# Attention and two mixture layers: filler products in the first head pairs, a common PSUM buffer for a product with phi, a later operand split, and transposes taken together

## The chip, the cores and the metric

The kernel runs on one core of one Trainium2 chip. What is measured is the device time of one execution in microseconds (us). The core has five engines with queues of their own: TensorE (PE in the rows, PEld for its weight loads), VectorE (DVE), ScalarE (ACT), GpSimd (POOL) and SyncE (SP), which here issues the transfers. 1.05 us is 0.2% of this kernel's time.

## The reference

Three layers follow each other: attention with a block-causal mask, a dense layer with a bent activation, and a soft mixture of eight experts with 32 slots in all.

```python
scores = scale * q @ k.T                          # 4 batches x 8 heads, 576 rows, head size 64
scores = where(row_block >= col_block, scores, -1e9)   # blocks of 64
x = softmax(scores) @ v                           # -> x: 2304 x 512
h = x @ w_in                                      # 512 x 2048
g = where(h >= 1, h, where(h <= -1, 0, (h + 1) ** 2 / 4))
x = g @ w_out                                     # 2048 x 512
logits = x @ phi                                  # 512 x 32
d = softmax(logits, over the tokens)
slot_input = d.T @ x                              # 8 experts x 4 slots x 512
slot_out = maximum(slot_input @ w1, 0) @ w2       # per expert, 512 x 1024 and 1024 x 512
out = softmax(logits, over the slots) @ slot_out
```

## The kernel before

**Attention** (about 0 to 200 us). There are 16 head pairs (a batch and two heads). The string `PLAN` is an order written out by hand: each of its tokens is a step of a pair, with a digit that says how many pairs behind the newest one it runs. Steps that matter here: `sc` are the score products of one row block (L113 for the diagonal one, L120 for the others), `mk` adds the mask to them with two small products (L126), `mx` takes the maximum on VectorE, `ex` the exponentials on ScalarE (L151), `no` scales the rows on GpSimd (L163), `pt` transposes them on TensorE (L171), `pc` copies them out. Scores lie in the PSUM pool `psc` (tag `sc`, two buffers of two banks), the transposes in the pool `ptr` (tag `tr`, three buffers of one bank).

**Blocks** (about 200 to 459 us). The tokens are five blocks, four of 512 and one of 256. `Moe.run` goes through a list of units k = 0, 1, ...; unit (b, f) computes 128 of the 2048 columns of h for block b: 12 products (L538, three for each of four parts of x, because both operands are split into a high and a low part), in a buffer of `ptr`, followed by the activation. The activation reads the buffer on ScalarE and last on VectorE (the maximum, L573), which frees it. The first 21 units alternate between blocks 0 and 1; then come 16 units each of block 2 (k = 21 to 36), 3 (37 to 52) and 4 (53 to 68). What else is done beside the units stands in a plan by unit:

- `w_parts` splits a tile of w_in into its two parts: a cast on ScalarE, then a subtraction and an addition on GpSimd (L484, L485). The tile is wanted by unit k's products some units later: w7 to w15 are made this way during the first units.
- `split(2)` splits x of block 2 in two halves, each a cast on ScalarE (L409) and two subtractions on GpSimd (L412). The first half is made ahead of the units, the second at k = 1 (`parts[1]()`).
- `wo_turn` transposes one tile of w_out (L498) in half of the buffer `aside`, which holds one of the two `psc` buffers through most of the block stage; ScalarE copies it out. After four tiles, `wo_phi` multiplies them with phi (L507, 16 products of 32 columns) and `wo_back` transposes the result (L516), both in that same half of `aside`, each with a copy by ScalarE (L511, L517). They run inside a unit, at k = 25 and 26, 30 and 31, 35 and 36, 40 and 41.
- `half(b, q, u)` transposes half u of a quarter of g of block b (L593, a `psc` buffer, copied out by ScalarE); with the second half of a quarter go its logits (`lt`, L613). `slots` multiplies them with the weights of the slots (L658), `soft`, `disp`, `weigh`, `maximum`, `weights` and `total` are the softmax pieces around it.
- `feed` issues the weights of the experts for the last stage as buffers come free.

**Experts** (about 459 to 521 us). A chain of small steps gives the slots' inputs, then the experts' two products run over weights that arrive by DMA. TensorE issues small filler products in its gaps there (L1015, bf16 128x128 zero operands).

The two places that the change touches first read:

```python
pairs[i].step(u)                      # L294
ps = self.aside[:, 1]                 # wo_phi and wo_back
if k == 1:
    parts[1]()
```

Of the kernel before, what the change touches and what calls it, by code (L numbers as in the profile page):

```python
# [7 lines left out]
F32 = mybir.dt.float32  # L8
# [6 lines left out]
P = 128  # L15
# [223 lines left out]

FILL = ""  # L240
WARM = 44

# [3 lines left out]
def attention(e, tc, nb=4, wl=(1, 1 + 2 * READY)):  # L248
    nc = tc.nc
    e.ENG = ENG  # L250

    def copy(eng, dst, src):
        if eng == "A":
            nc.scalar.copy(dst, src)  # L254
        elif eng == "D":
            nc.vector.tensor_copy(dst, src)
        else:
            nc.gpsimd.tensor_scalar(out=dst, in0=src, scalar1=1.0, scalar2=1.0, op0=ALU.mult, op1=ALU.mult)
    e.copy = copy
    e.eng = lambda c: nc.vector if c == "D" else nc.gpsimd  # L260

    e.QD, e.pr, e.v_, e.acc = [], [], [], []
    for i in range(2):
        e.QD.append(e.apool.tile([P, 2, P], F32R, tag=f"QD{i}", bufs=1, name=f"QD{i}"))
        z = (nc.gpsimd, nc.vector)[i]
        z.memset(e.QD[i][0:64, :, 64:P].bitcast(F32), 0.0)
        z.memset(e.QD[i][64:P, :, 0:64].bitcast(F32), 0.0)
        e.pr.append([e.apool.tile([P, P * (b // 2 + 1)], F32, tag=f"pr{i}{b}", bufs=1, name=f"pr{i}{b}")
                     for b in range(9)])
        z.memset(e.pr[i][8][:, 576:640], 0.0)  # L270
        e.v_.append(e.apool.tile([P, 5, 2, 64], F32, tag=f"natv{i}", bufs=1, name=f"vn{i}"))
        z.memset(e.v_[i][64:P, 4], 0.0)
    for i in range(2):
        e.acc.append(e.apool.tile([P, 16, 2], F32, tag=f"acc{i}", bufs=1, name=f"ac{i}"))
        nc.vector.memset(e.acc[i], 1e-9)
    e.low = e.apool.tile([P, P], mybir.dt.bfloat16, tag="low", bufs=1, name="low")
    e.one = e.apool.tile([P, 64], mybir.dt.bfloat16, tag="one", bufs=1, name="one")
    nc.vector.memset(e.low, 0.0)
    nc.vector.memset(e.one, 1.0)
    for h in (0, 64):  # L280
        nc.vector.memset(e.low[h:h + 1, 0:64], -2.0 ** 127)
    pairs = [Pair(e, nc, b, p) for b in range(nb) for p in range(4)]
    n = len(pairs)
    plan = [(it - int(u[0]), u[1:]) for it in range(n + 6) for u in PLAN.split()]
    plan = [(i, u) for i, u in plan if ((i, int(u[2:])) in EARLY if u[0] == "h" and u[1] in "mxyzoa" else
                                        0 <= i < n if u[0] != "w" else wl[0] <= i < wl[1])]
    fill = [(int(u[0]), u[1:]) for u in FILL.split()]
    assert sorted(fill) == sorted(plan[:len(fill)])
    for i, u in fill + plan[len(fill):]:
        if u[0] == "h":  # L290
            e.moe.early(u[1], *EARLY[i, int(u[2:])])
        elif u[0] != "w":
            pairs[i].step(u)
        else:  # L294
            t, c = (i - wl[0]) // 2, slice((i - wl[0]) % 2 * 256, (i - wl[0]) % 2 * 256 + 256)
            if u == "w0" and c.start == 0:
                e.moe.w_raw(t)
            elif u == "w1":
                e.moe.w_mul(t, c)
                e.moe.w_bits(t, c)  # L300
            elif u == "w2":
                e.moe.w_parts(t, c, e.ENG["w"])
# [14 lines left out]
class Moe:  # L317
# [183 lines left out]

    def wo_phi(self, c):
        e, nc = self.e, self.nc
        ps = self.aside[:, 1]
        for kk in range(4):
            for i in range(4):
                nc.tensor.matmul(ps[32 * i:32 * i + 32, 0:P], e.phi[:, kk], self.wT[2 * c + i // 2][:, i % 2, kk],  # L507
                                 start=(kk == 0), stop=(kk == 3))
        self.drop(f"wT{4 * c}", f"wT{4 * c + 2}")
        wp = self.wp = e.y[:, 3]  # L510
        nc.scalar.copy(wp, ps[:, 0:P])  # L511

    def wo_back(self, c):
        e, nc = self.e, self.nc
        ps = self.aside[:, 1]
        nc.tensor.transpose(ps[:, 0:P], self.wp, e.ident)  # L516
        nc.scalar.copy(e.w2p[:, 4 * c:4 * c + 4].rearrange("p i s -> p (i s)"), ps[:, 0:P])  # L517

# [311 lines left out]
    def plan_sides(self, at_unit):  # L830
# [6 lines left out]
        def put(k, name, *a):  # L837
            at.setdefault(k, []).append((name, *a))
            return k
        for f in range(16):  # L840
            k = put(prep[first + f] + 2, "wo_turn", f)
            if f % 4 == 3:
                c = f // 4
# [11 lines left out]
            put(free + 2 * b + 2, "weigh", b)  # L855
        free += 2
        at_half = {}
        for b in range(2, 4):
            for q in range(4):
                for u in range(2):  # L860
                    free = put(max(free + 1, pos(b, 4 * q + 3) + 2), "half", b, q, u)
                    at_half.setdefault((b, q), free)
            if b == 2:
                put(free, "soft", 2)
                for i, step in enumerate((("disp", 2), ("weigh", 2), ("logits", 3, range(8)))):
                    put(free + 1, *step)
                for i, step in enumerate((("slots", 2, 0), ("logits", 3, range(8, 16)), ("soft", 3))):
                    put(free + 2, *step)
                put(free + 3, "slots", 2, 1)
                put(free + 4, "disp", 3)  # L870
                put(free + 6, "maximum")
                put(free + 7, "weights")
                put(free + 8, "weigh", 3)
        put(at_half[3, 1] + 2, "slots", 3, 0)
        put(free + 1, "slots", 3, 1)
        put(free + 2, "total")
        for q in range(3):
            k = put(max(pos(4, 4 * q + 3) + 3, free + 1 + q), "half", 4, q, 0)
        put(k, "gather")
        for b in range(2, 5):  # L880
            for u, fn in enumerate(self.split(b)):
# [11 lines left out]
    def run(self):  # L893
# [23 lines left out]
        for k, (b, f) in enumerate(units):  # L917
            for i in [READY + n for n, p in enumerate(prep) if p == k - 1]:
                self.w_parts(i)
            for i in [READY + n for n, p in enumerate(prep) if p == k > 0]:  # L920
                self.w_mul(i)
                self.w_bits(i)
            if k == 1:
                parts[1]()
            for i in [READY + n for n, p in enumerate(prep) if max(p - 2, 0) == k and n > 1]:
                self.w_raw(i)
            self.h_unit(b, f, at.pop(-k, ()) if k else ())
            self.act_unit(b, f, "D" if k > prep[-1] or k < 18 and k % 2 else "A")
            for fn, *a in at.pop(k, []):
                (getattr(self, fn) if isinstance(fn, str) else fn)(*a)  # L930
            if k == 66:
                self.n4 = self.new([P, 4, 256], F32R, "n4")
                for i in range(4):
                    self.comb_parts(i)
            if k == 57:
                self.middle, self.spare = len(self.tape), 1
            if k > 29:
                self.feed()
# [306 lines left out]
```

## Time and profile before

| | |
|---|---|
| median of 3 runs | 523.71 us (523.31 to 523.95) |
| the profiled execution | 523.28 us |
| its span, first to last instruction | 521.5 us |
| TensorE busy | 500.6 us (96%) |
| VectorE, ScalarE, GpSimd busy | 331.6, 327.0, 203.9 us |
| mean granted clock of TensorE | 0.980 |

The profile is one execution. TensorE is busy nearly all the time, so the time is read from three things: where it waits (the view of the waits and the timeline), at which granted clock it works (the column PEclk of a stretch; 1.00 is 2.4 GHz, 0.50 is 1.2 GHz), and how many products it has. The timeline gives for each instruction its start, its length and, in brackets, the idle time of the engine before it and what ended that.

### The profile page before, as it was taken

What the parts mean: (1) busy time and instruction counts of PE and PEld (TensorE: products, weight loads), DVE (VectorE), ACT (ScalarE), POOL (GpSimd) and SP (SyncE); (2) the same over time, 40 slices, a digit from 0 to 9 for tenths busy, and PEclk for the clock granted to TensorE, in tenths of its full rate; (3) what the DMA queues carried; (4) which work ended last, traced back from release to release, by engine and by line L of the source; (5) the groups of instructions that cost most, each with busy time, mean ns of one, the idle gap of its engine ahead of it and who ended that gap; (6) DMA issues with size and microseconds to landing.
All of it is one profiled execution on the core that took longest, in us unless ns stands there. A gap on an engine that the chain in (4) does not pass through costs nothing.

```text
span 521.5 us, 11780 instructions
## 1 busy us (share of the span) xinstructions
PE 500.6 (96%) x4504; PEld 384.5 (74%) x4504; DVE 331.6 (64%) x672; ACT 327.0 (63%) x734; POOL 203.9 (39%) x264
## 2 busy tenths in 40 slices
PE   6799999999999999899999999899999999999994
PEld 5678887888888887688887887788767978753453
DVE  6879988888887655888888545833463444431232
ACT  4889998888887645557787888643333535452131
POOL 3888997777777424744523212600002000000000
PEclk8789999999999999899999999999999999999998
DMA  6235334343321155111257865341075679979997
GB/s 204 92 95 167 115 99 142 88 125 98 91 52 29 53 163 215 53 43 61 101 168 236 288 235 184 110 154 41 5 277 175 222 253 412 391 237 373 411 412 308
DMA packets 42711, 91.01 MB, mean 175 GB/s; under 512 B 8736, under 2 KB 18080, under 8 KB 42656
## 3 DMA queue, kind: packets, MB, share of 16 engines
q1 hardware_dynamic: 42656, 90.26, 51.0%
q8 instruction: 36, 0.59, 0.4%
q14 instruction: 19, 0.16, 0.1%
HBM read 74.51 MB, written 14.68 MB: 171 GB/s over the span
## 4 chain that ended last, share of the span: by engine, by line
PE 81%; ACT 4%; DMA 3%; DVE 3%; issue 1%; POOL 1%; SPq 0%; ACTq 0%; DVEq 0%; POOLq 0%
PE h L538 33%; PE sc L120 7%; PE gn L593 5%; PE om L189 5%; PE s L658 3%; PE eh L1031 3%; PE ps_1p L171 2%; PE sc L113 2%; PE lt L613 2%; PE ps_2p L171 2%; PE ps_3p L171 2%; PE acc L1058 2%; PE om L194 2%; PE ps_0p L171 2%; DMA ew<-in_w2b_dram 1%
## 5 line engine op out<-in xcount | busy, mean ns | idle before, releaser
L538 PE MATMUL h<-xh,w 128*128 128x512 f32 (+1 forms) x384 | 115.2, 368 | 0.0
L538 PE MATMUL h<-xt,w 128*128 128x512 f32 x384 | 101.2, 408 | 1.6 <-POOL w L485 1.4
L163 POOL TENSOR_SCALAR pr<-pr,sm 128x512 f32<-128x512 f32 (+2 forms) x144 | 88.7, 633 | 24.7 <-DVE sm L158 23.0
L151 ACT ACTIVATE pr<-sc,nm 128x512 f32<-128x512 f32 (+2 forms) x144 | 78.3, 551 | 10.1 <-DVE nm L146 8.6
L538 PEld LDWEIGHTS h<-xt,w 128*128 128x128 f32 x384 | 69.5, 191 | 16.2 <-POOL w L485 2.7
L572 DVE SCALAR_TENSOR_TENSOR g<-g 128x512 f32<-128x512 f32 (+1 forms) x52 | 37.6, 724 | 65.6 <-ACT g L559 65.6
L538 PEld LDWEIGHTS h<-xh,w 128*128 128x128 f32 x384 | 69.0, 189 | 13.8 <-issue 3.8
L538 PE MATMUL h<-xl,w 128*128 128x512 f32 (+1 forms) x192 | 68.1, 355 | 0.0
L146 DVE TENSOR_REDUCE nm<-sc 128x2 f32<-128x1024 f32 (+1 forms) x64 | 52.3, 818 | 21.2 <-PE sc L126 20.9
L573 DVE TENSOR_TENSOR g<-h,g 128x512 f32<-128x512 f32 (+1 forms) x80 | 50.9, 636 | 15.8 <-ACT g L564 13.7
L559 ACT ACTIVATE g<-h,half 128x512 f32<-128x512 f32 (+1 forms) x52 | 32.3, 622 | 43.1 <-PE h L538 41.5
L120 PE MATMUL sc<-K,Q 64*128 64x512 f32 (+3 forms) x384 | 47.8, 363 | 3.7 <-ACT pr L151 2.7
L689 POOL TENSOR_TENSOR cn<-cn,cm 128x128 f32<-128x128 f32 (+1 forms) x5 | 1.9, 378 | 124.7 <-DVE cm L688 124.7
L254 ACT COPY gn<-gn 128x1024 f32<-128x1024 f32 x35 | 35.3, 1009 | 13.1 <-PE gn L593 12.7
L120 PEld LDWEIGHTS sc<-K,Q 64*128 64x128 f32 x384 | 30.2, 196 | 14.0 <-issue 5.6
L538 PEld LDWEIGHTS h<-xl,w 128*128 128x128 f32 x192 | 36.4, 189 | 3.8
L477 POOL TENSOR_TENSOR wab<-wab 128x512 f32<-128x512 f32 x16 | 21.0, 1312 | 44.0 <-DVE wab L469 23.3
L593 PE MATMUL gn<-ident,g 128*128 128x128 f32 x280 | 36.7, 274 | 0.2 <-ACT gn L254 0.2
L593 PEld LDWEIGHTS gn<-ident,g 128*128 128x128 f32 x280 | 31.7, 140 | 6.7 <-issue 2.1
L484 POOL TENSOR_TENSOR wab<-wab,w 128x256 f32<-128x256 f32 (+1 forms) x23 | 23.2, 1010 | 22.5 <-ACT w L254 21.3
L467 DVE SCALAR_TENSOR_TENSOR wab<-wab 128x512 uint32<-128x512 uint32 (+1 forms) x39 | 25.4, 651 | 10.0 <-ACT wab L460 6.6
L561 ACT ACTIVATE g<-h,half 128x512 f32<-128x512 f32 x28 | 19.3, 689 | 19.9 <-PE h L538 15.8
(226 smaller groups left out, 892.1 us busy)
## 6 DMA issues: line engine op xcount, KB each, us to landing
ew<-in_w_dram SPq DMA_DIRECT2D x32, 512.0 KB, 6.8
raw<-in_w_in_dram SPq DMA_DIRECT2D x16, 512.0 KB, 5.3
raw<-in_w_out_dram SPq DMA_DIRECT2D x16, 512.0 KB, 4.3
ew<-in_w2a_dram SPq DMA_DIRECT2D x16, 510.0 KB, 8.8
ew<-in_w2b_dram SPq DMA_DIRECT2D x16, 344.0 KB, 6.7
kn<-in_k_dram SPq DMA_DIRECT2D x16, 288.0 KB, 3.2
qn<-in_q_dram SPq DMA_DIRECT2D x16, 288.0 KB, 4.3
vn<-in_v_dram SPq DMA_DIRECT2D x16, 256.0 KB, 3.3
```

The source lines that it names most:

```text
L120: nc.tensor.matmul(sc[:, h, 0:n], self.Q[r, qa, 128 * i:128 * i + 128], self.K[r, ka, 0:n], start=(k == 0), stop=False)
L146: nc.vector.tensor_reduce(out=self.negm[:, 2 * i:2 * i + 2], in_=self.scs[i][:, :, 0:128 * (i + 1)], axis=AX.X, op=ALU.max, negate=True)
L151: self.nc.scalar.activation(pr, sc, AF.Exp, bias=self.negm[:, b:b + 1], accum_out=self.acc[:, b, 0:1])
L163: self.nc.gpsimd.tensor_scalar(out=pr, in0=pr, scalar1=self.sums[:, b:b + 1], scalar2=1.0, op0=ALU.mult, op1=ALU.mult)
L171: nc.tensor.transpose(ps[:, u * P:(u + 1) * P], self.pr[b][:, kc * P:(kc + 1) * P], e.ident)
L189: nc.tensor.matmul(om[64 * h:64 * h + 64, (t0 - ts[0]) * P:len(ts) * P], self.v[:, kc, h, :], self.PT[:, a:a + 2 * n - 1:2], start=(kc == ...
L254: nc.scalar.copy(dst, src)
L538: nc.tensor.matmul(ph[:, 0:n], w[:, wi, kk], self.x(b, kk, xi)[:, 0:n], start=(kk + m == 0), stop=(kk + m == 5))
L559: nc.scalar.activation(g, ph, AF.Relu, bias=e.half[:, 0:1], scale=0.5)
L572: nc.vector.scalar_tensor_tensor(out=g, in0=g, scalar=1.0, in1=g, op0=ALU.min, op1=ALU.mult)
L573: nc.vector.tensor_tensor(out=g, in0=ph, in1=g, op=ALU.max)
L593: nc.tensor.transpose(ps[:, j, i * P:(i + 1) * P], self.gt(b, f)[:, o:o + P], e.ident)
```

## The change

**Filler products.** A table `KEEP` gives for ten steps `mk` of the pairs 0, 1 and 2 a number of products of the zero tile with itself (bf16, 128x128), 70 in all. They are issued on TensorE right behind the mask products of that step, into a buffer of `ptr` that nobody reads.

**phi in the common buffers.** `wo_phi` and `wo_back` take a buffer of `ptr` in place of the half of `aside`.

**The split of block 2.** Its second half is made at k = 3 in place of k = 1.

**Halves together.** In `plan_sides` both halves u = 0 and 1 of a quarter of blocks 2 and 3 are put at one unit: for block 2 at k = 48, 49 (the first quarter, as before), 51, 53 and 55, for block 3 at 58, 60, 62 and 64. With them move `slots` 2 1 (58 to 57), `slots` 3 0 (60 to 61), `slots` 3 1 (64 to 65), `maximum` (61 to 60), `total` (65 to 66), and the first halves of block 4, all three to 66 (before: 64, 65, 66).

```diff
+KEEP = {(0, "mk2"): 20, (0, "mk1"): 6, (0, "mk0"): 2, (1, "mk3"): 6, (1, "mk2"): 6, (1, "mk1"): 13, (1, "mk0"): 2,
+        (2, "mk3"): 5, (2, "mk2"): 5, (2, "mk1"): 5}
...
             pairs[i].step(u)
+            if (i, u) in KEEP:
+                keep = e.ptr.tile([P, 512], F32, tag="tr", name=f"keep{i}{u}")
+                for _ in range(KEEP[i, u]):
+                    nc.tensor.matmul(keep[:, 0:P], e.zero, e.zero, start=True, stop=True)
...
     def wo_phi(self, c):
-        ps = self.aside[:, 1]
+        ps = e.ptr.tile([P, 512], F32, tag="tr", name=f"ph{c}")
...
     def wo_back(self, c):
-        ps = self.aside[:, 1]
+        ps = e.ptr.tile([P, 512], F32, tag="tr", name=f"bk{c}")
...
-                for u in range(2):
-                    free = put(max(free + 1, pos(b, 4 * q + 3) + 2), "half", b, q, u)
...
+        for q in range(4):
+            for u in range(2):
+                free = put(max(free + (2 * (1 - u) if q else 1), pos(2, 4 * q + 3) + 2), "half", 2, q, u)
...
+        for q, k in enumerate((3, 5, 7, 9)):
+            for u in range(2):
+                put(max(free + k, pos(3, 4 * q + 3) + 2), "half", 3, q, u)
         for q in range(3):
-            k = put(max(pos(4, 4 * q + 3) + 3, free + 1 + q), "half", 4, q, 0)
+            k = put(max(pos(4, 4 * q + 3) + 3, free + 11), "half", 4, q, 0)
...
-            if k == 1:
+            if k == 3:
                 parts[1]()
```

The order of TensorE's instructions in the first head pair, before, from the scores of its third block on (`sc0_02` and so on are scores of pair 0; `low` is the mask's tile):

```order
L120 MATMUL sc0_02_238<-K_0_0_211,Q_0_0_218 128x384 x6
L126 LDWEIGHTS low_199
L126 MATMUL sc0_02_238<-one_200,low_199 128x64
L126 LDWEIGHTS low_199
L126 MATMUL sc0_02_238<-one_200,low_199 128x64
L113 MATMUL sc0_04_266<-K_0_0_211,QD0_165 128x288 x6
L120 MATMUL sc0_01_274<-K_0_0_211,Q_0_0_218 128x256 x6
```

After (warm is the tile of zeros, `keep0mk2` the buffer that nobody reads):

```order
L120 MATMUL sc0_02_238<-K_0_0_211,Q_0_0_218 128x384 x6
...
L126 LDWEIGHTS low_199
L126 MATMUL sc0_02_238<-one_200,low_199 128x64
L299 LDWEIGHTS warm_69
L299 MATMUL keep0mk2_247<-warm_69 128x128
L299 LDWEIGHTS warm_69
L299 MATMUL keep0mk2_247<-warm_69 128x128
...
L299 LDWEIGHTS warm_69
L299 MATMUL keep0mk2_247<-warm_69 128x128
L113 MATMUL sc0_04_287<-K_0_0_211,QD0_165 128x288 x6
```

The 20 products now stand between the mask of block 2 and the diagonal scores; nothing else moved there.

GpSimd's order at the start of the block stage, before (`xl20` and `xl21` are the low parts of block 2's halves, `w7` to `w9` the tiles of w_in):

```order
L412 TENSOR_TENSOR xl20_3054<-xw20_148,xh20_3053 128x512 x2
L484 TENSOR_TENSOR wab7_3047<-wab7_3047,w7_3076 128x512
L485 TENSOR_TENSOR w7_3076<-wab7_3047 128x512
L412 TENSOR_TENSOR xl21_3081<-xw21_149,xh21_3080 128x512 x2
L484 TENSOR_TENSOR wab8_3101<-wab8_3101,w8_3130 128x512
L485 TENSOR_TENSOR w8_3130<-wab8_3101 128x512
L484 TENSOR_TENSOR wab9_3150<-wab9_3150,w9_3175 128x512
```

After:

```order
L418 TENSOR_TENSOR xl20_3134<-xw20_148,xh20_3133 128x512 x2
L490 TENSOR_TENSOR wab7_3127<-wab7_3127,w7_3156 128x512
L491 TENSOR_TENSOR w7_3156<-wab7_3127 128x512
L490 TENSOR_TENSOR wab8_3176<-wab8_3176,w8_3205 128x512
L491 TENSOR_TENSOR w8_3205<-wab8_3176 128x512
L418 TENSOR_TENSOR xl21_3210<-xw21_149,xh21_3209 128x512 x2
L490 TENSOR_TENSOR wab9_3230<-wab9_3230,w9_3255 128x512
```

The subtractions of `xl21` moved from ahead of the split of w8 to behind it, and so ahead of that of w9.

TensorE's order around the first product with phi, in unit k = 25 (`h2_4`) and at the start of the next, before (`wT` are the transposed tiles of w_out):

```order
L538 MATMUL h2_4_3685<-xl21_3081,w4_1619 128x512
L538 MATMUL h2_4_3685<-xh21_3080,w4_1619 128x512
L507 MATMUL aside_3042<-wT0_3552,phi_123 32x128 x2
L507 MATMUL aside_3042<-wT2_3612,phi_123 32x128 x2
...
L538 MATMUL h2_4_3685<-xh21_3080,w4_1619 128x512
L538 MATMUL h2_4_3685<-xl21_3081,w4_1619 128x512
L538 MATMUL h2_4_3685<-xh21_3080,w4_1619 128x512
L498 MATMUL aside_3042<-ident_116,wab20_3618 128x128 x4
L538 MATMUL h2_5_3736<-xh20_3053,w5_1986 128x512
```

After (`ph0` is a buffer of `ptr`, taken between those of `h2_4` and `h2_5`):

```order
L544 MATMUL h2_4_3765<-xl21_3210,w4_1699 128x512
L544 MATMUL h2_4_3765<-xh21_3209,w4_1699 128x512
L513 MATMUL ph0_3775<-wT0_3632,phi_123 32x128 x2
L513 MATMUL ph0_3775<-wT2_3692,phi_123 32x128 x2
...
L544 MATMUL h2_4_3765<-xh21_3209,w4_1699 128x512
L544 MATMUL h2_4_3765<-xl21_3210,w4_1699 128x512
L544 MATMUL h2_4_3765<-xh21_3209,w4_1699 128x512
L504 MATMUL aside_3122<-ident_116,wab20_3698 128x128 x4
L544 MATMUL h2_5_3817<-xh20_3133,w5_2066 128x512
```

No product moved; the product with phi has left `aside`, in which the transposes of `wab20` stay, and takes its turn among the buffers of the units.

TensorE's order at the second quarter of block 2, before (`gn210` and `gn211` are the buffers of its two halves, `h3_14` is a unit of block 3, `lt2` are logits):

```order
L593 MATMUL gn210_4824<-ident_116,g2_4_4630 128x128 x2
L593 MATMUL gn210_4824<-ident_116,g2_6_4680 128x128 x2
...
L538 MATMUL h3_14_4844<-xh30_4148,w14_3406 128x512
L538 MATMUL h3_14_4844<-xl30_4149,w14_3406 128x512
...
L538 MATMUL h3_14_4844<-xl31_4231,w14_3406 128x512
L538 MATMUL h3_14_4844<-xh31_4230,w14_3406 128x512
L593 MATMUL gn211_4861<-ident_116,g2_4_4630 128x128 x2
L593 MATMUL gn211_4861<-ident_116,g2_6_4680 128x128 x2
...
L613 MATMUL lt2_4773<-g2_4_4630,w2p_3041 32x128 x8
L613 MATMUL lt2_4773<-g2_6_4680,w2p_3041 32x128 x8
```

After:

```order
L544 MATMUL h3_14_4921<-xl31_4316,w14_3486 128x512
L544 MATMUL h3_14_4921<-xh31_4315,w14_3486 128x512
L599 MATMUL gn210_4938<-ident_116,g2_4_4768 128x128 x2
L599 MATMUL gn210_4938<-ident_116,g2_6_4813 128x128 x2
...
L599 MATMUL gn211_4949<-ident_116,g2_4_4768 128x128 x2
L599 MATMUL gn211_4949<-ident_116,g2_6_4813 128x128 x2
...
L619 MATMUL lt2_4861<-g2_4_4768,w2p_3121 32x128 x8
L619 MATMUL lt2_4861<-g2_6_4813,w2p_3121 32x128 x8
L544 MATMUL h3_15_4980<-xh30_4232,w15_3531 128x512
```

The first half moved one unit later, to stand directly ahead of the second.

## Rows read from the trace of the kernel before

**Rows 1.** TensorE's waits over the span: operation, releaser, us, times, longest.

```profile
PE sc L120 <- ACT pr L151: 2.7, 4, 1.5
...
PE h L538 <- POOL w L485: 1.4, 1, 1.4
PE aside L498 <- ACT w2p L517: 1.4, 1, 1.4
...
PE aside L498 <- ACT y L511: 1.0, 1, 1.0
```

**Rows 2.** Four stretches: length, then busy of each engine, PEclk, DMA share, GB/s.

```profile
9.40:19.70 10.30, 7.77 (x42) 5.82 (x42) 7.56 (x18) 7.57 (x25) 7.08 (x10) 0.50 0.44 120
26.50:29.90 3.40, 3.40 (x20) 1.98 (x17) 2.16 (x4) 2.63 (x10) 3.40 (x5) 0.50 0.67 171
217.60:221.00 3.40, 3.40 (x9) 2.65 (x8) 1.75 (x4) 1.21 (x3) 2.56 (x2) 0.51 0.32 90
326.90:333.70 6.80, 5.39 (x27) 4.17 (x26) 5.96 (x7) 5.13 (x9) 5.09 (x4) 1.00 0.10 39
```

**Rows 3.** Timeline of pairs 0 to 2: start, length, operation, idle before.

```profile
11.07 1.78 PE L113 MATMUL sc<-K,QD 128*128 128x288 f32 x6 [2.20 <-ACT pr L151]
...
12.89 0.76 DVE L144 TENSOR_REDUCE nm<-sc 128x1 f32<-128x576 f32 x1 [0.39 <-PE sc L113]
...
15.71 1.65 PE L120 MATMUL sc<-K,Q 64*128 64x512 f32 x6 [0.17 <-ACT pr L151]
...
18.74 0.69 ACT L151 ACTIVATE pr<-sc,nm 128x512 f32<-128x512 f32 x1 [1.49 <-DVE nm L146]
...
25.91 1.16 PE L120 MATMUL sc<-K,Q 64*128 64x512 f32 x6 [0.31 <-ACT pr L151]
...
27.66 0.50 PEld L171 LDWEIGHTS ps_1p<-ident,pr 128*128 128x128 f32 x3 [0.29 <-POOL pr L163]
```

**Rows 4.** Timeline of TensorE in the tail: the kernel's own filler products.

```profile
510.10 0.72 PE L1015 MATMUL gap<-warm 128*128 128x128 bf16 x10
```

**Rows 5.** Timeline, start of the block stage: the splits of block 2 and w8.

```profile
204.97 0.63 ACT L564 ACTIVATE g<-g 128x512 f32<-128x512 f32 x1
...
208.81 3.18 POOL L412 TENSOR_TENSOR xl<-xw,xh 128x512 fp32r<-128x512 f32 x2
...
210.46 0.63 ACT L564 ACTIVATE g<-g 128x512 f32<-128x512 f32 x1
...
214.94 1.60 POOL L485 TENSOR_TENSOR w<-wab 128x512 fp32r<-128x512 f32 x1
...
216.60 0.73 PE L538 MATMUL h<-xt,w 128*128 128x512 f32 x2 [1.43 <-POOL w L485]
```

**Rows 6.** Timeline at the first and the third phi product.

```profile
282.68 0.68 DVE L573 TENSOR_TENSOR g<-h,g 128x512 f32<-128x512 f32 x1
...
283.62 0.48 PE L538 MATMUL h<-xh,w 128*128 128x512 f32 x1
...
332.85 1.47 POOL L477 TENSOR_TENSOR wab<-wab 128x512 f32<-128x512 f32 x1
...
334.76 0.60 PE L498 MATMUL aside<-ident,wab 128*128 128x128 f32 x4
```

**Rows 7.** Timeline of TensorE at two slot steps of blocks 2 and 3.

```profile
419.88 1.92 PE L658 MATMUL s<-gn,y 128*32 128x512 f32 x16
421.62 1.93 PE L613 MATMUL lt<-g,w2p 128*32 128x128 f32 x64
...
425.93 1.92 PE L658 MATMUL s<-gn,y 128*32 128x512 f32 x16
427.79 1.09 PE L593 MATMUL gn<-ident,g 128*128 128x128 f32 x8
```

**Rows 8.** Two stretches near the end of the blocks, columns as in rows 2.

```profile
440.00:450.00 10.00, 10.00 (x91) 7.61 (x93) 5.16 (x14) 4.39 (x8) 0.40 (x1) 1.00 1.02 407
450.00:460.00 10.00, 10.00 (x90) 7.58 (x82) 3.76 (x13) 5.54 (x12) 0.00 (x0) 1.00 0.79 297
```

More of the change, by code (lines that the diff above doesn't have):

```diff
@@ L857, in plan_sides @@
         at_half = {}
-        for b in range(2, 4):
-            for q in range(4):
-                for u in range(2):
-                    free = put(max(free + 1, pos(b, 4 * q + 3) + 2), "half", b, q, u)
[L862 to L876, printed above, removed]
+        for q in range(4):
+            for u in range(2):
+                free = put(max(free + (2 * (1 - u) if q else 1), pos(2, 4 * q + 3) + 2), "half", 2, q, u)
+                at_half.setdefault((2, q), free)
+        put(free, "soft", 2)
+        for k, *step in ((1, "disp", 2), (1, "weigh", 2), (1, "logits", 3, range(8)), (2, "slots", 2, 0), (2, "slots", 2, 1),
+                         (2, "logits", 3, range(8, 16)), (2, "soft", 3), (4, "disp", 3), (6, "slots", 3, 0), (5, "maximum"),
+                         (7, "weights"), (8, "weigh", 3), (10, "slots", 3, 1), (11, "total")):
+            put(free + k, *step)
+        for q, k in enumerate((3, 5, 7, 9)):
+            for u in range(2):
+                put(max(free + k, pos(3, 4 * q + 3) + 2), "half", 3, q, u)
         for q in range(3):
-            k = put(max(pos(4, 4 * q + 3) + 3, free + 1 + q), "half", 4, q, 0)
+            k = put(max(pos(4, 4 * q + 3) + 3, free + 11), "half", 4, q, 0)
         put(k, "gather")
```

## Prediction

> **What bounds the kernel now.** TensorE does: it is busy 10.00 of 10.00 us late in the block stage and 3.40 of 3.40 in the other stretches without a wait [rows 8, 2]. So the first view to read is the one of TensorE's waits, which says how much can be had at all: 2.7 and 2.2 us in the first head pairs, 1.4 on GpSimd's split of a w_in tile, 1.4 and 1.0 at the transposes of w_out [rows 1, 3]. The second is the granted clock by stretch. It was at 0.5 (1.2 GHz) in 9.4 to 19.7, 26.5 to 29.9 and 217.6 to 221.0 us, and at 1.0 (2.4 GHz) around them [rows 2]. Ahead of each fall TensorE had waited: 2.20 us before 11.07 [rows 3], up to 1.5 before the second [rows 1], 1.43 before 216.60 [rows 5]. A wait costs twice where such a stretch follows it, but not every wait did that: a wait of 1.41 us lies in 326.9 to 333.7, which stayed at 1.00 [rows 1, 2]. The last view is the share of the DMA engines, for the pieces of the expert stage: 1.02 in 440 to 450, 0.79 in 450 to 460 [rows 8].
>
> All steps below are against the profiled execution, 523.28 us (span 521.5, 1.78 around it); the median is 0.43 above it. They are taken off the median.
>
> **Zero products in the first pairs.** 70 products are added. The tail of this kernel issues the same kind: ten took 0.72 us with their last one's latency [rows 4], so about 0.06 each at full clock and, as an estimate, 0.12 at half. The 20 of pair 0's second block stand where TensorE waited 2.20 us for ScalarE [rows 3]: 1.2 us of it is filled and 1.0 stays. If the clock then holds at full, this follows. The diagonal scores at 11.07, 1.78 us at half clock, take about 1.0; VectorE's maximum of them at 12.89 had waited 0.39 for them and starts that much earlier [rows 3]. ScalarE's exponentials follow it, and they release the scores of pair 1: 15.71 becomes 15.3, and these take about 0.9 in place of 1.65. VectorE's maximum and ScalarE's exponentials behind them, at 18.74 with 1.49 us idle, come 0.4 + 0.7 = 1.1 earlier [rows 3]. From there ScalarE runs nearly without idle time up to pair 2, whose first scores wait 0.31 for it at 25.91 [rows 3]; they come about 1.0 earlier. The 28 products of pair 0 and 27 of pair 1 lie in TensorE's idle time (10.30 − 7.77 = 2.5 us at half clock [rows 2], more at full), so I cost them nothing; if that cover is gone, the next paragraphs' rivals have the price. From 25.91 on TensorE sets the pace itself. The stretch 26.5 to 29.9 holds 3.40 us of work at half clock [rows 2], 1.7 at full: 1.7 saved, less pair 2's 15 products, which now stand on the path (15 x 0.06 = 0.9), less some 0.4 because the transposes of pair 2 then arrive ahead of GpSimd, for which their weight load waited 0.29 already [rows 3]. Sum 1.0 + 1.7 − 0.9 − 0.4 = **1.4 gained**. Ends: 1.9 (no wait for GpSimd) and a loss of 0.9, where nothing of the clock is won and the 15 products are paid; 1.8 lost if they run at half clock.
>
> **The split two units later.** Today GpSimd takes the two subtractions of the second half of block 2 (208.81, 3.18 us) ahead of the split of w8, whose last part ends at 214.94 + 1.60 = 216.54; TensorE waits 1.43 for it at 216.60 [rows 5] and then loses 3.4 / 2 = 1.7 more at half clock [rows 2]. After the change both parts of w8 stand ahead of those subtractions and w8 is in time. But the same pattern comes back two units on: ScalarE's cast for the split, behind the activations of unit 2 in place of unit 0, starts where those end, 211.09 in place of 205.60 [rows 5], 5.5 us later, so the last part of w9 ends near 216.54 + 5.5 = 222.0. TensorE wants w9 two units after w8, and the activations of two units at its pace lie those same 5.5 us apart [rows 5]. So the wait of 1.43 us is handed from w8 to w9 nearly whole, and w10 behind it has time again. What hangs on it is the clock: 1.43 was followed by the half clock, 1.41 elsewhere was not. I take the fall as likelier than not, since this wait lies in the same work as the one that was followed by it: **0.0 gained**. Ends: 3.1 (no wait and no fall), 1.8 (wait, no fall), and a loss of 0.3 if the cast, which ScalarE now does behind a unit of three activations, falls later.
>
> **The phi product and its turn in the common buffers.** The two waits, 1.41 and 0.99 us [rows 1], are for copies by ScalarE out of the one buffer that the transposes of w_out share; they go. What is late next? The phi product takes one of the three buffers through which h units pass, so the unit behind it starts only when VectorE's maximum of the unit before is done. At the first phi (k 25 and 26) that is 282.68 + 0.68 = 283.36, where the unit starts at 283.62 now [rows 6]: of the 0.99 only about 0.2 is kept. At the third, the transpose of the next w_out tile needs GpSimd's addition, 332.85 + 1.47 = 334.32, which stands behind the subtractions of block 3; it runs at 334.76 now [rows 6]: 0.4 kept of 1.41. The second and fourth had no wait and get none. Sum **0.6 gained**; ends 0 and 2.4.
> Perfetto Trace Analysis, a page of the Trainium skill, says in its section Matmuls that independent groups of products should go round different PSUM banks, so that emptying one runs beside the next group. By that the whole 2.4 us would go, 1.8 more than my sum; the rows 6 say that the wait for the buffer turns into one for VectorE and GpSimd.
>
> **Both halves at one place.** The products are the same, in another order. Going from the slot products over to logits took 421.62 − 419.88 = 1.74 us, over to transposes 427.79 − 425.93 = 1.86 [rows 7]: a change between products that use 32 columns and such that use the whole array costs about 0.1, and standing the two slot steps of block 2 together spares two: **0.2 gained**. What could be late is ScalarE's copy of the first half, since the slot step or half behind the second asks for that buffer again, and the totals, which follow the last slot step by one unit; the products of an h unit stand between in both places. Ends a gain and a loss of 0.4, twice my value. SP issues the expert pieces by room, up to three of them one unit later than now at two places, while the queue is full (share 1.02); 0.79 in 450 to 460 leaves 2 us of room behind it [rows 8], so I cost it at nothing. The expert stage then moves forward as a whole, since its later pieces are released by TensorE's own progress; if its transfers did not move along, 2 us at most would be lost of the gain.
>
> **Sum**: 1.4 + 0.0 + 0.6 + 0.2 = 2.2, so 523.7 − 2.2 = **521.5 us**, with 520.6 to 522.4 for this case alone.
>
> **Rivals.**
> *The clock stays up at w9.* For: a wait of 1.41 us in 326.9 to 333.7 was not followed by the half clock [rows 1, 2]. Against: the one of 1.43 at 216.60 was [rows 5, 2], and it is this very wait that moves. 1.7 more: 519.8.
> *The waits at w_out go altogether*: the common buffers come round in time, because VectorE's maxima and GpSimd's additions also move forward by then. For: the ScalarE work ahead of them does. Against: the margins of 0.2 and 0.4 in rows 6. 1.8 more: 519.7. The Trainium skill's Perfetto Trace Analysis, Matmuls, speaks for this case.
> *The products do not hold the clock* (the change does not do what it says). For: 1.0 us stays open ahead of the diagonal scores, and a similar gap behind them. Against: 1.41 us in 326.9 to 333.7 had no half clock behind it [rows 1, 2]. Then pair 1's 1.0 us and the 1.7 stay lost, and the 15 products of pair 2 cost 0.9 to 1.8: 523.7 − 0.8 (the other parts) + 0.9 = 523.8, up to 524.7.
> *The products delay the transposes behind them* (slower). They stand in TensorE's order ahead of the transposes of pairs 1 and 2, for which ScalarE and GpSimd wait. From the point at which pair 1's scores run at half clock, 12 products of pair 1 and 15 of pair 2 at 0.12 are 3.2 us on the path: 523.7 − 0.8 + 3.2 = 526.1. For: 10.3 us at half clock hold 7.77 of work there [rows 2], room for no more than 2.5. Against: the 2.20 that brought the clock down is halved.
>
> **How the numbers follow.** Forecast 0.40, clock up at w9 0.23, waits at w_out gone 0.09, clock not held 0.20, transposes delayed 0.08. A measurement of this kernel can tell about 0.2% (1.05 us) from no change: below 522.66 is faster, above 524.76 slower. The first three cases are faster (0.72), the fourth the same (0.20), the last slower (0.08). The range goes from 519.2, just under the two faster rivals, to 523.9, the middle of the fourth case; outside it lie the last case, half of the fourth at most, and little below.
>
> **What would show it.** In the profile after: a granted clock of 1.0 from 7 to 33 us, and pair 2's first scores at about 24.9, show the first step; a half clock there shows the third rival. A wait of h on GpSimd's L491 of about 1.4 us two units later than now shows the second, and a stretch at 0.5 behind it parts forecast and first rival. For phi: no wait on ScalarE's copies, and in their place short ones on VectorE's maximum near unit 26 and on GpSimd near unit 37. For the halves: no new wait on ScalarE or VectorE from 380 us on. Wrong it would be above all if the clock fell at another place, which no sum over instructions shows.

## The result, and the profile after

The kernel after takes 517.95 us at the median of 4 executions (517.23 to 518.37), the kernel before 523.83 (523.31 to 524.22): a ratio of 0.9887 with an interval of 0.9870 to 0.9904, 5.9 us less where 2.2 were forecast and 519.2 was the lower end of the range. The profiled execution takes 518.23 us with a span of 516.4, which is 5.1 us less than the span before.

The page of the kernel after: its span, TensorE's busy time, and TensorE's granted clock in 40 equal slices.

```profile
span 516.4 us, 11910 instructions
...
PE 499.3 (97%) x4574; PEld 384.5 (74%) x4574; DVE 331.3 (64%) x672; ACT 326.5 (63%) x734; POOL 204.8 (40%) x264
...
PEclk9999999999999999999999999999999999999998
```

No slice but the last has less than nine tenths of the clock. The waits of TensorE, with the columns of [rows 1]:

```profile
PE sc L120 <- ACT pr L151: 1.7, 2, 0.9
PE h L544 <- POOL w L491: 1.4, 1, 1.4
...
PE sc L113 <- ACT pr L151: 1.0, 1, 1.0
...
PE h L544 <- POOL xl L418: 0.7, 1, 0.7
...
PE h L544 <- DVE g L579: 0.5, 1, 0.5
```

Of the waits before, that of pair 0's diagonal scores is down from 2.2 [rows 3] to 1.0 and those of the other scores from 2.7 to 1.7 in all; that on a w_in tile is as long as it was; the two at the transposes of w_out [rows 1] are gone, and two shorter ones, on GpSimd and on VectorE, are there in their place. The stretches that answer to [rows 2], the last two around the wait on w9:

```profile
9.40:19.70 10.30, 8.37 (x90) 6.79 (x88) 8.95 (x21) 8.98 (x29) 8.43 (x13) 1.00 0.49 138
26.50:29.90 3.40, 3.40 (x35) 3.20 (x35) 2.97 (x8) 3.15 (x10) 3.26 (x6) 1.00 0.64 178
217.80:221.20 3.40, 1.96 (x9) 1.22 (x8) 3.23 (x6) 2.11 (x5) 2.17 (x2) 1.00 0.47 154
221.20:224.60 3.40, 3.40 (x17) 2.79 (x16) 2.81 (x5) 1.83 (x3) 2.65 (x2) 1.00 0.01 2
```

The clock stays at 1.00 in all of them, also in the 3.4 us behind the wait. The first pairs, in answer to [rows 3]:

```profile
11.00 1.03 PE L113 MATMUL sc<-K,QD 128*128 128x288 f32 x6 [0.97 <-ACT pr L151]
...
12.35 0.73 DVE L144 TENSOR_REDUCE nm<-sc 128x1 f32<-128x576 f32 x1
...
14.91 0.97 PE L120 MATMUL sc<-K,Q 64*128 64x512 f32 x6
...
17.22 0.69 ACT L151 ACTIVATE pr<-sc,nm 128x512 f32<-128x512 f32 x1 [0.75 <-DVE nm L146]
...
24.24 0.97 PE L120 MATMUL sc<-K,Q 64*128 64x512 f32 x6
```

The diagonal scores take 1.03 us in place of 1.78. Pair 1's first scores come 0.8 us earlier (14.91 for 15.71), ScalarE behind them 1.5 (17.22 for 18.74), and pair 2's first scores 1.67 (24.24 for 25.91); the forecast had 0.4, 1.1 and 1.0. GpSimd and TensorE at the split, in answer to [rows 5]:

```profile
212.29 3.19 POOL L418 TENSOR_TENSOR xl<-xw,xh 128x512 fp32r<-128x512 f32 x2
...
218.45 1.60 POOL L491 TENSOR_TENSOR w<-wab 128x512 fp32r<-128x512 f32 x1
...
220.10 4.16 PE L544 MATMUL h<-xt,w 128*128 128x512 f32 x17 [1.44 <-POOL w L491]
```

As forecast the subtractions come behind the split of w8, and the wait, 1.44 for 1.43, falls on w9.

To see where the time went, the span is cut at the ends of VectorE's maxima (a maximum is the last instruction of a unit). The first pairs reach up to the first maximum, which belongs to a unit done early in attention. Then come units 0 to 10, which hold the wait on w8 or w9, units 22 to 42 with the phi products, 42 to 68 with the halves, and the rest. From the first maximum to unit 0 it is 118.1 to 118.2 us in every profile but one (below), and units 10 to 22 take 33.9 to 34.0 us in every kernel of the table. The rows are in microseconds, worked out from the timeline of one execution each:

| kernel | first pairs | 0 to 10 | 22 to 42 | 42 to 68 | rest |
|---|---|---|---|---|---|
| before | 88.16 | 31.20 | 86.63 | 102.31 | 61.06 |
| after | 86.22 | 29.63 | 85.76 | 102.23 | 60.56 |
| products alone (p_keep) | 86.76 | 31.25 | 86.15 | 102.31 | 60.30 |
| split alone (p_split) | 87.08 | 29.63 | 85.82 | 102.31 | 60.38 |
| phi alone (p_phi) | 89.69 | 29.62 | 85.65 | 102.30 | 61.96 |
| halves alone (p_halves) | 90.36 | 29.60 | 86.49 | 102.23 | 62.55 |
| after without products (m_keep) | 91.21 | 29.63 | 86.20 | 102.24 | 60.85 |
| after, split at k = 1 (m_split) | 85.25 | 31.22 | 85.58 | 102.22 | 60.47 |
| after, phi as before (m_phi) | 86.42 | 29.63 | 85.73 | 102.23 | 60.60 |
| after, halves apart (m_halves) | 87.55 | 29.63 | 85.09 | 102.31 | 60.56 |

By the two profiled executions alone the first pairs gave 1.9 us, the stretch of the split 1.6, phi 0.9, the halves 0.1 and the rest 0.5. The rows below them show how far one execution may be trusted: without the zero products the first pairs are the same code in five profiles, and take from 87.1 to 91.2 us.

### The profile page after: what moved, and what is told of

The parts are those of the page before. It is cut to its first block, busy times and chain, and to the rows that moved or that the text cites. A ratio compares the mean times of both kernels' runs of the same rounds, so it can differ in the third digit from the quotient of the medians.

```text
span 516.4 us, 11910 instructions
## 1 busy us (share of the span) xinstructions
PE 499.3 (97%) x4574; PEld 384.5 (74%) x4574; DVE 331.3 (64%) x672; ACT 326.5 (63%) x734; POOL 204.8 (40%) x264
## 4 chain that ended last, share of the span: by engine, by line
PE 82%; ACT 5%; DMA 4%; DVE 4%; POOL 2%; issue 2%; SPq 0%; ACTq 0%; DVEq 0%; POOLq 0%
PE h L544 33%; PE sc L120 7%; PE gn L599 5%; PE om L189 5%; PE s L664 3%; PE eh L1030 3%; PE sc L113 2%; PE lt L619 2%; PE ps_2p L171 2%; PE ps_1p L171 2%; PE ps_3p L171 2%; PE ps_0p L171 2%; PE acc L1057 2%; PE om L194 2%; DMA ew<-in_w2b_dram 1%
## 5 line engine op out<-in xcount | busy, mean ns | idle before, releaser
L544 PE MATMUL h<-xt,w 128*128 128x512 f32 x384 | 99.7, 403 | 1.4 <-POOL w L491 1.4
L544 PEld LDWEIGHTS h<-xt,w 128*128 128x128 f32 x384 | 68.3, 188 | 15.8 <-POOL w L491 3.1
L120 PE MATMUL sc<-K,Q 64*128 64x512 f32 (+3 forms) x384 | 45.1, 347 | 2.9 <-ACT pr L151 1.7
L120 PEld LDWEIGHTS sc<-K,Q 64*128 64x128 f32 x384 | 28.5, 186 | 13.0 <-issue 5.3
L599 PE MATMUL gn<-ident,g 128*128 128x128 f32 x280 | 35.3, 273 | 0.0
L490 POOL TENSOR_TENSOR wab<-wab,w 128x256 f32<-128x256 f32 (+1 forms) x23 | 23.3, 1011 | 20.4 <-ACT w L256 19.2
```

The lines of the kernel that those rows point to most:

```text
L120: nc.tensor.matmul(sc[:, h, 0:n], self.Q[r, qa, 128 * i:128 * i + 128], self.K[r, ka, 0:n], start=(k == 0), stop=False)
L544: nc.tensor.matmul(ph[:, 0:n], w[:, wi, kk], self.x(b, kk, xi)[:, 0:n], start=(kk + m == 0), stop=(kk + m == 5))
L599: nc.tensor.transpose(ps[:, j, i * P:(i + 1) * P], self.gt(b, f)[:, o:o + P], e.ident)
```

## Experiments: each part alone

**The products alone.** Edit: `KEEP` and the loop behind `pairs[i].step(u)`, in the kernel before.

> The kernel before with the 70 zero products alone. Two theories on the clock at the start of the blocks. A, that moving the split keeps it up: here the split is where it was, so after the gain of 2.0 us in the first pairs the wait of 1.4 us on w8 is again followed by half clock, 523.8 - 2.0 = 521.8. B, that it is the place of the wait in time: everything lies 2.0 us earlier here, the same wait of 1.4 us has no half clock behind it, 521.8 - 1.7 = 520.1.

Measured: 519.23 us against 523.86, a ratio of 0.9914 (0.9887 to 0.9941): 4.6 us, from 3.1 to 5.9. So this part is most of the change. Both theories miss: the median lies 0.9 below B's 520.1, but the profiled execution (520.62) has half clock behind the wait on w8, as A has it. Its stretches of the wait and behind it, columns as in [rows 2]:

```profile
212.40:215.80 3.40, 1.83 (x8) 0.90 (x7) 3.26 (x5) 2.60 (x4) 2.67 (x2) 1.00 0.01 2
215.80:219.20 3.40, 3.40 (x10) 2.64 (x9) 2.15 (x4) 0.62 (x1) 2.16 (x2) 0.50 0.21 47
```

**The split alone.**

```diff
-            if k == 1:
+            if k == 3:
                 parts[1]()
```

> The kernel before with the split of block 2 at k = 3 alone. The wait of 1.4 us goes from w8 to w9 in either theory. A: no half clock behind it, 523.8 - 1.7 = 522.1. B: whether the clock falls hangs on where the wait lies in time, and it lies elsewhere than in the kernel after (2 us later), so a fall as in the kernel before is as likely, 523.8, and 522.1 would be no evidence for either.

Measured: 523.80 us, a ratio of 0.9994 (0.9966 to 1.0021); its 12 executions lie between 519.1 and 526.4, so 1 us either way would not be seen here, and neither theory is ruled out by the time. The profiled one waits 1.44 us for w9 with no half clock behind it.

**phi in the common buffers alone.** Edit: the two lines `ps = self.aside[:, 1]` as in the change.

> The kernel before with the phi product and its turn in the common buffers alone. By the two traces the waits of 2.4 us turn into waits of 0.5 on VectorE and 0.7 on GpSimd, a gain of 0.9, 522.9. The rival, that common buffers let all waits go and those left come with the other parts: 2.4, 521.4.

Measured: 523.20 us, a ratio of 0.9986 (0.9968 to 1.0005), 0.7 us less, near the first theory; the interval still holds no change at all, but not the rival's 521.4. TensorE's waits in its profile:

```profile
PE h L538 <- POOL w L485: 1.4, 1, 1.4
...
PE h L538 <- POOL xl L412: 0.7, 1, 0.7
PE h L538 <- DVE g L573: 0.6, 1, 0.6
```

The two waits at the w_out transposes are gone, and 0.7 and 0.6 stand in for them on GpSimd and VectorE without any other part of the change. The stretch from unit 22 to 42 takes 85.65 us, and 86.63 before.

**The halves alone.** Edit: `plan_sides` as in the change.

> The kernel before with the halves together alone. By the two traces the blocks gain 0.1 us, 523.7. The rival, that the 0.5 us by which the last expert weights came earlier still is due to the pieces' new places in the queue: 523.2. Slower, by up to 0.4, if the copies of the halves come late.

Measured: 523.68 us, a ratio of 0.9994 (0.9976 to 1.0012); the stretch from unit 42 on is 0.08 us shorter. The rival on the expert pieces finds nothing for it: the rest of the span takes 62.55 here.

## Experiments: the change less one part

**Less the products.** `KEEP = {}` in the kernel after.

> The kernel after without the zero products. Theory C: the products are worth about 4.5 us at the median, because in the first pairs of the kernel before the half clock takes anything from 10 to 20 us of an execution, longer mostly than in the one profiled; the other parts together are worth 0.6 to 1.3. Then 522.6 to 523.2, and the last maximum of the first pairs lies near 88 to 90 us in the trace. Rival (the sum of the two traces): the products are worth 2.0, the split's place 1.6, so 520.0.

Measured: 523.45 us against 523.69, a ratio of 0.9975 (0.9948 to 1.0001). So the products are worth 5.5 us as the last part (523.45 less 517.95). The median is near theory C's 522.6 to 523.2 and far from the 520.0 of the two traces, but its 12 executions spread from 519.03 to 525.21, five of them below 521.1. The stretches of the first pairs in its profile show where the time is in a long one:

```profile
7.80:21.40 13.60, 10.89 (x59) 8.16 (x60) 9.71 (x19) 8.35 (x26) 9.51 (x13) 0.50 0.43 125
28.30:35.10 6.80, 6.69 (x31) 5.68 (x32) 4.87 (x10) 4.92 (x13) 4.67 (x9) 0.50 0.51 136
```

That is 20.4 us at half clock, where the execution in [rows 2] had 13.7 in these pairs. It runs the same first pairs as the kernel before, and they take 3.0 us longer.

**Less the split's move.** `if k == 1:` in the kernel after.

> The kernel after with the split of block 2 back at k = 1. Theory C: the wait of 1.4 us stands at w8 in place of w9 and the half clock follows it in some executions and not in others, as it would at w9: 518.0, the same within 0.5. Theory A (the place of the split keeps the clock up): 1.7 slower, 519.6, with half clock behind the wait.

Measured: 519.02 us, a ratio of 0.9910 (0.9888 to 0.9933), 1.1 above the kernel after, with half clock behind the wait in the profiled execution. That speaks for A and against C, though the intervals overlap. Over all profiles the count is clearer: with the split at k = 1 the half clock follows the wait in 3 of 5 (before, p_keep and m_split; not p_phi and p_halves), with the split at k = 3 and a wait of 1.43 to 1.48 us in none of 9.

The waits are equally long, so what differs? The weight load ahead of the wait, in this kernel:

```profile
211.53 0.30 PEld L544 LDWEIGHTS h<-xt,w 128*128 128x128 f32 x2 [0.54 <-ACT wab L466]
...
213.69 2.80 PE L544 MATMUL h<-xt,w 128*128 128x512 f32 x7 [1.43 <-POOL w L491]
```

and in the kernel after:

```profile
217.93 0.30 PEld L544 LDWEIGHTS h<-xt,w 128*128 128x128 f32 x2 [0.32 <-ACT wab L466]
```

Ahead of the wait at k = 1 stands a second one of 0.54 us; at k = 3 it is 0.32. The products' starts there are 0.53 us apart in place of 0.31. So TensorE is idle for some 0.2 us more around the same wait. This alone does not decide: p_phi and p_halves have the same 0.54 and 1.43 us and no half clock behind them.

**Less phi, less the halves.** The two `ps` lines, or `plan_sides`, as before.

> The kernel after with the phi product and its turn back in the buffer of the w_out transposes: the stage from unit 22 to unit 42 takes 86.2 to 86.6 us in place of 85.7, so 0.6 slower, 518.6. The rival, that with the first pairs faster the old buffer's waits are hidden: 518.0.

> The kernel after with the halves apart again: 0.1 slower, 518.1; the stage from unit 42 to 68 takes 102.3 us in place of 102.2. The rival, that the order of the expert pieces matters for the last stage: 0.5 either way.

Measured: 518.84 us (0.9905, 0.9887 to 0.9923), 0.9 slower than the kernel after, and 518.00 (0.9890, 0.9870 to 0.9910), the same. In the table the five executions with phi in `aside` take 86.16 us on average from unit 22 to 42, the five with the common buffers 85.66: 0.5 gained, though single rows overlap. The profile without the phi part (85.73) is no longer than the kernel after, against my expectation; but the two waits on ScalarE's copies are back in it, 1.0 us each, where the kernel after has 0.7 and 0.5 on GpSimd and VectorE.

## Experiments on the clock

**Products of some pairs only.** `KEEP` with pair 0's entries alone (28 products), and with pairs 1 and 2 alone (42).

> The kernel after with pair 0's 28 zero products alone. If the wait of 2.2 us in pair 0 is what brings the clock down for long, nearly all of the gain stays, and pair 2's 15 products, which cost 0.9 on the path, are gone: 517 to 518. If the wait of 1.5 us in pair 1 brings it down in its turn, 1.7 more: 519 to 520.

> The kernel after with the 42 products of pairs 1 and 2 alone. If pair 0's wait decides, the clock falls there as in the kernel before and the 27 products of pair 1 run at half clock ahead of the transposes: 522 to 524. If the products of pair 1 bring it up again at once, 520.

Measured: 519.28 us (0.9906, 0.9879 to 0.9933) and 521.01 (0.9932, 0.9907 to 0.9957). Pair 0 alone, from the first scores on:

```profile
6.00:24.80 18.80, 14.10 (x137) 10.72 (x137) 15.22 (x33) 15.30 (x48) 14.86 (x21) 1.00 0.42 134
24.80:28.20 3.40, 3.38 (x16) 2.32 (x17) 2.72 (x5) 2.22 (x8) 3.40 (x5) 0.50 0.74 186
```

Pairs 1 and 2 alone:

```profile
9.90:20.10 10.20, 8.41 (x49) 6.42 (x50) 6.75 (x16) 7.47 (x25) 7.25 (x10) 0.50 0.39 104
20.10:33.00 12.90, 12.03 (x124) 10.26 (x122) 10.78 (x24) 11.26 (x33) 10.83 (x18) 1.00 0.42 131
```

With pair 0 filled the clock holds there and falls in pair 1, behind a wait of 1.84 us; with pair 0 empty it falls at 9.9, 1.6 us into pair 0's wait of 2.52. In these two executions each group of products keeps the clock up where it stands, and pair 0's are worth more, since the clock is down for 10.2 us there and 3.4 in pair 1. The mean clocks of all six executions of each agree with that order: 0.988 to 0.997 with pair 0 filled, 0.985 to 0.989 with pair 0 empty.

**A longer wait at k = 3.** GpSimd clears part of a buffer that it overwrites next, for w9 alone; three lengths (`(384,)`, `(384, 208)`, `(512, 512)`):

```diff
+        if i == 9:
+            for c9 in (384, 208):
+                p.memset(w[:, 1, 0:c9].bitcast(F32), 0.0)
         p.tensor_tensor(out=w[:, 1], in0=A, in1=B, op=ALU.add)
```

> The kernel after with one more GpSimd instruction, some 0.4 us of clearing a buffer that is overwritten next, between the two parts of the split of w9: the wait becomes about 1.8 us. If the idle time of TensorE decides on the half clock, it now follows the wait in half of the executions or more, and the median is 518.0 + 0.4 + about 1 = 519.4. If the place of the split decides, the clock stays up: 518.4.

Measured: 518.06 us (0.9903, 0.9873 to 0.9934). It does not part the two cases: the wait became only 1.48, because the next GpSimd instruction took 1.27 us in place of 1.60.

> As the last one with a longer wait on w9, with 0.65 us of clearing in place of 0.43: a wait of about 1.75 us, which with the 0.1 ahead of it is as much idle time as at k = 1. If the idle time decides, half clock behind it in half of the executions: 518.0 + 0.3 + 0.8 = 519.1. If the place decides: 518.3.

> The same with 1.0 us of clearing: a wait of about 2.1 us, nearly the 2.2 of pair 0. If the idle time decides, half clock in most executions: 518.0 + 0.65 + 1.4 = 520.0. If the place decides: 518.65.

Measured: 520.50 us (0.9921, 0.9895 to 0.9946) with a wait of 1.79, and 520.92 (0.9920, 0.9892 to 0.9948) with one of 2.15: 2.5 and 3.0 above the kernel after, where the waits alone are 0.35 and 0.7 longer. The kernel before, measured beside them, was slower too (524.51 for 523.83), so by the ratios it is some 1.8 and 1.7 us, and the intervals overlap that of the kernel after. The longest one's wait, and the stretches of it and behind it:

```profile
221.65 2.98 PE L547 MATMUL h<-xt,w 128*128 128x512 f32 x9 [2.15 <-POOL w L494]
```

```profile
219.70:223.10 3.40, 1.46 (x6) 1.24 (x7) 3.23 (x5) 1.63 (x3) 1.79 (x2) 1.00 0.30 118
223.10:226.50 3.40, 3.40 (x9) 2.67 (x9) 2.01 (x4) 1.48 (x3) 2.88 (x2) 0.50 0.00 0
```

So the place of the split alone does not keep the clock up: in this execution the half clock comes at k = 3 too, behind a longer wait. The profiled execution of the middle one (517.2 span), whose wait is 1.79, has none behind it. That the 0.2 us of idle time is what parts k = 1 from k = 3 fits these runs, but is not shown by them.

**The price of a product on the path.** 15 more in each of pairs 6, 8 and 10, at the steps of pair 2.

> The kernel after with 45 more zero products, 15 in each of pairs 6, 8 and 10, at the steps at which pair 2 has its own. At the sum's price of 0.06 us, all on the path: 518.0 + 2.7 = 520.7. If TensorE's order has room for them there: 518.0.

Measured: 520.23 us (0.9942, 0.9920 to 0.9964), 2.3 above the kernel after. Its profile is the one whose time from the first pairs to unit 0 differs: 119.91 in place of 118.15, 1.76 us for 45 products, 0.04 each.

## Tries for a better kernel

The split at k = 17: `if k == 17:`.

> The kernel after with the second split of block 2 at k = 17, where GpSimd has no split of a w_in tile left to do. If the wait of 1.4 us is handed on only because GpSimd has no free time in the first units, it vanishes here, and with it any half clock behind it: 518.0 - 1.4 = 516.6, less where the half clock would have followed. Rival: the subtractions then hold up GpSimd's additions for w_out or the products of block 2, and as much is lost there: 518.0.

Measured: 518.35 us (0.9888, 0.9863 to 0.9913). The wait on w9 is gone (27.87 us from unit 0 to 10), but the next stretch, units 10 to 22, takes 36.13 in place of 33.90: the rival was right, GpSimd now makes the transposes of w_out wait.

```profile
PE sc L113 <- ACT pr L151: 1.8, 1, 1.8
PE aside L504 <- POOL wab L483: 1.7, 4, 0.8
```

The same with `WARM = 58` and a `KEEP` of 32, 16 and 2 in pair 0, 6, 6, 24 and 2 in pair 1, and none in pair 2:

> A try for a better kernel: the split at k = 17, 14 more warm products ahead of the first scores, 12, 10 and 11 more where 1.0, 0.8 and 0.9 us of waiting are left in pairs 0 and 1, and none in pair 2. If the half clock in the first pairs hangs on the waits that are left, no execution falls there any more, and pair 2's 15 products are saved: 0.5 to 1.5 below the kernel with the split at k = 17, 515 to 516. Rival: the added products stand ahead of scores that come early in some executions and cost what they save: 516.6.

Measured: 518.13 us (0.9880, 0.9854 to 0.9905). This is no gain over the one before.

The split's two subtractions at two places (the second at k = 5):

```diff
+                sub(0)
+                if (i, u) == (2, 1):
+                    self.later = rest
```

> The kernel after with the split's first subtraction at k = 3 and its second at k = 5. If the wait comes from two subtractions in one stretch, which slow VectorE's steps for the next tile, each alone leaves TensorE no wait or a short one: 518.0 - 1.4 = 516.6. Rival: each costs half of it at its own tile, twice 0.7: 518.0.

The last one with the `WARM` and `KEEP` of the try before it:

> The same with 14 more warm products ahead of the first scores, 12, 10 and 11 more zero products in pairs 0 and 1, and none in pair 2: equal to the one before within 0.5 if pair 2's 15 products cost little or the clock falls without them, 0.9 faster if they are paid in full.

Measured, in this order: 517.60 us (0.9892, 0.9862 to 0.9921) and 517.62 (0.9882, 0.9853 to 0.9912). The wait splits in two, 0.7 and 0.3, and the stretch from unit 0 to 10 takes 29.03 in place of 29.63. None of the four can be told from the kernel after. In all 12 executions of the two with more `WARM` and `KEEP` the mean clock is 0.994 or more, and their two profiles have no half clock but at the end of the span; that they are no faster suggests that the half clock which the table leaves in the first pairs costs about as much as the products that remove it.

## Why the prediction was wrong

**The zero products: the term was mis-sized, 1.4 for 4.6 (3.1 to 5.9).** The direction held: the scores of pairs 1 and 2 and the exponentials between them came earlier one behind the other. In the two profiled executions this chain gave 1.67 us up to pair 2's first scores where the sum had 1.0, and 1.94 up to the end of the first pairs where it had 1.4. Part of the latter is the price of a product on the path: 0.04 us in pairs 6, 8 and 10 and not 0.06, by which, as an estimate, pair 2's 15 cost 0.6, 0.3 less than the sum took off.

The rest was a matter of what the clock does in other executions. "If the clock then holds at full" is not what the products bring about, and the wait named for the first fall was not the one: the clock fell at 9.4, only some 0.5 us into the 2.20 us that ended at 11.07 [rows 2, 3]. TensorE had already waited 1.03 us for the first scores, and in p_keep, where it was 1.88, the clock fell behind that wait, at 7.6, ahead of the first zero product (9.80). The first scores before, and then those of p_keep with the stretch behind them:

```profile
6.89 1.29 PE L120 MATMUL sc<-K,Q 64*128 64x512 f32 x6 [1.03 <-ACT Q L89]
```

```profile
7.00 1.59 PE L120 MATMUL sc<-K,Q 64*128 64x512 f32 x6 [1.88 <-ACT Q L89]
```

```profile
7.60:11.00 3.40, 3.35 (x26) 2.54 (x25) 2.43 (x4) 1.47 (x4) 1.41 (x1) 0.50 0.47 97
```

In m_keep, without the products, the clock fell at the same place and stayed down for 13.6 us in place of 3.4. So what the products change is also how long it stays down. Of the 11 profiles with the whole table (the kernel after and ten more) seven have half clock in the first pairs, 3.4 us in six and 6.8 in one; four of the five without it have 10.2 to 20.5. In the fifth, p_halves, the record of the clock begins only at 20.5 us, and pair 0's diagonal scores ahead of that take 1.78 us, as they do at half clock. The 11 need 86.7 us on average for the first pairs, from 85.2 to 88.0, and the five 89.3, from 87.1 to 91.2: 2.6 us for the 1.4 of the sum.

Was it bad luck with the execution that the sum stood on? Only in part. Its first pairs, 88.2 us, are the second shortest of the five. But its mean granted clock, 0.980, is that of the median execution: (1 − 0.98) x 2 x 521.7 = 20.9 us at half clock, against 5.2 in the median execution of the kernel after (both counted to the end of the span, where TensorE has nothing left to do).

Beside the 2.6 us, about 0.7 of the 4.6 lies in the rest of the span, where its end varies with the last transfers. The remaining 1.3 are not found in the averages. A likely place is the wait on w8, though no profile shows it: every profile has 3.1 to 6.1 us of half clock at its end, and two of the six executions of p_keep had 3.1 and 5.2 us in all by their mean clocks (0.997 and 0.995), which leaves no room for a further 3.4 behind that wait. The profiled one, which has it, is the second slowest of the six.

**The split: the wait right, the clock wrong.** The wait was handed on whole, to 0.01 us and to the two units. I took the fall of the clock behind it as likelier than not, because a wait of the same length was followed by one before. That step failed: in none of nine profiles did the clock fall behind the new wait, and the old one brought it down in three of five only. I compared the waits by their listed length and did not look at the weight load ahead of them, which waits 0.54 us at the old place and 0.32 at the new; whether this is the cause stays open, since two of the five have the 0.54 and no fall. The rival that the clock stays up at w9 is what happened. It is worth about 1.1 us at the median (the kernel after against the one with the split at k = 1, whose intervals overlap), less than the 1.7 it was priced at; that fits an old place that brought the clock down in a part of the executions. Two ends of ranges in the prediction are 0.1 too high by its own terms: 1.0 + 1.7 − 0.9 is 1.8, and 3.4 / 2 is 1.7. The forecast does not hang on them.

**phi: right in size.** 0.5 to 0.9 us were gained for 0.6, in the profiles and at the medians, where the intervals do not part it from no change. The wait on VectorE stands where it was forecast, the one on GpSimd at the subtractions of block 3 and not at the addition behind them:

```profile
276.37 0.50 PE L544 MATMUL h<-xh,w 128*128 128x512 f32 x1 [0.49 <-DVE g L579]
...
328.89 0.50 PE L544 MATMUL h<-xl,w 128*128 128x512 f32 x1 [0.72 <-POOL xl L418]
```

The section Matmuls of the Trainium skill's Perfetto Trace Analysis says that where independent groups of products go round different PSUM banks, emptying one overlaps the next group. The trace agrees in part: of the 2.4 us of waits half came back, 0.5 on VectorE, which empties the common buffers, and 0.7 on GpSimd, whose subtractions make an operand of the products.

**The halves: right, and smaller.** The stretch gave 0.08 us for the 0.2 forecast; nothing came late. The time of the kernel cannot show so little.

**The expert stage** moved forward as a whole: the last weight transfer on the chain is issued at 496.80, 5.0 us earlier than before, and still ends the chain.

```profile
496.80 6.77 DMA ew<-in_w2b_dram
```

With the two clock terms at their measured size (4.6 and 1.1) beside 0.6 and 0.1 the sum is 6.4 us, against 5.9 (5.0 to 6.8) measured. The two may count the half clock behind the old wait twice.

## What to carry to other kernels

A stretch at half clock in one profile is a sample: before it is priced, look at several executions, by their times and by more than one profile, and price the change against their average. The mean granted clock helps, but it can be too high: p_halves's 0.989 leaves out the first 20.5 us. A few products of zeros cost 0.04 us each on the path here, and 70 of them inside TensorE's early waits gave 4.6 us; look at every wait ahead of the fall, also the one for the first operands. Moving work on a busy engine can hand its wait to the next tile whole; compare the old and the new place by all the idle time around the wait, and in more than one execution.

## What the runs showed of the hardware

The granted clock did not follow the same wait in every execution: behind the 1.43 us on w8 it fell to 0.50 in three profiles and stayed at 1.00 in two, with the same 0.5 us of the weight load ahead of the wait in each. GpSimd's last addition for w9 took 1.60 us in the kernel after and 1.27 behind 0.43 us of clearing. A VectorE instruction was still running for the first 0.47 us of the one and the first 0.11 of the other, which fits the difference but is not tested. Where the 0.5 us by which the sum and the measured gain still differ lies, the share of executions in which a given wait brings the clock down, and what decides it stay open.
